# Delta-rule attention, gMLP and rotor mixer on one core: r and u products on four array tiles, a third Gram buffer, masked query parts by DRAM

## The chip, the core and the metric

The kernel runs on one core of a Trainium2 chip. Its engines are TensorE (PE; PEld is its loading of weights), VectorE (DVE), ScalarE (ACT), GpSimd (POOL) and SyncE (SP, which issues the transfers here). The metric is device time of the whole program in microseconds (us), the lower the better; the median of three runs is compared.

## The reference

Three layers follow each other on B=4 sequences of 768 tokens. The first is a delta rule per head (8 heads of 48), which as written goes token by token:

```python
k_n = k / (norm(k) + 1e-06)
for t in range(S):
    y[:, :, t] = q[:, :, t] @ state
    v_old = k_n[:, :, t] @ state
    state += beta * outer(k_n[:, :, t], v[:, :, t] - v_old)
# second: gated MLP; third: token and channel mixing
h = relu(x @ w_in); u, v = split(h); v_n = layernorm(v)
x = (u * (w_spatial @ v_n + b_spatial)) @ w_out
theta = x @ w_theta
y = w_tok_r @ (x * cos(theta)) + w_tok_i @ (x * sin(theta))
u = x + y
out = u + relu(u @ w_ch)
```

## The kernel before

The attention is done in chunks of 64 tokens. A *step* g (0 to 47) is one chunk of one sequence with all 8 heads, four head pairs (`hp`) that lie in partitions 0 to 63 and 64 to 127. Twelve steps make a sequence, eight steps make a *round* r (0 to 5). Per step there are:

- `gram` (L660): the products of the chunk's keys with each other (and, from round 2 on, with its queries) go to PSUM tile `gp`, are multiplied with `gm` (causal mask times beta and norm, made on POOL in `gmask`) on DVE and give `GX` (keys) and `pp` (masked query part). In rounds 0 and 1 the query part is made one step ahead in `jit` (L803), straight into `kq`.
- `norms` (L609), once a round: the norms of the keys, a row of seven small DVE instructions in one task `f2`.
- `invert` (L712), once a round: the 32 unit triangular matrices of the round are inverted together. 30 levels of two DVE instructions (`tmp`, L746; `un`, L758) invert 32x32 blocks after a transpose (L724) and before two (L763, L766); then 32x32 products on PE with PSUM tile `mg` (L784, L790), `MU`=8 matrices at a time, give the blocks below.
- `chain` (L839): PE product r (L858, L859: keys by state `w`), DVE `rt` = r - v (L862), PE product u (L869, L870: inverse by `rt`), two copies to `w`, PE product s (L885, L887: keys by u, summed onto the state), two copies to the next `w`, and PE product y (L897, L898: the output). r, rt, u, s of a step wait for one another, and the next step's r for s.

r and u take 8 matmuls of 64x64 (or 48x64) weights and 48 columns a step. Head 0 of a pair goes to one output half and head 1 to the other, so that two of the four 64x64 tiles of the array are in use. As the operands are fp32, each matmul shows as two records in the trace.

Two buffers `GX` hold the rounds' matrices: round r+2 uses that of round r, so `gram` of step g+16 stands behind `chain` of step g, and `invert` of round r+2 behind the last step of round r.

The big matmuls of the other two layers (`mm_tasks`, L987, recorded at L998) are done for a sequence once its attention is there. A planner (`Plan`) lists all tasks with a priority and assumed durations and writes out every engine's order before the program is built; on the chip each engine runs its list in order and waits on semaphores. It puts big matmuls between the small products of the chain, and where too few are ready it puts in *fillers* (L508): 128x128 transposes whose result is not read, so that TensorE stays busy. They write a corner of PSUM tile `mg`. `park` (L1162) turns the third layer's weights from float64 pairs into fp32 in DRAM, 34 pieces, from step 16 on.

```python
        marks[g] = A(o_pe(480), fu, [rt, G], [pu], pr, crit=True, act=0.312)
```

This line adds the u product as a PE task with an assumed 480 ns.

## Time and profile before

| | |
|---|---|
| median of 3 runs | 806.61 us (800.92 to 808.93) |
| the profiled execution, its own time | 808.53 us |
| its span, first to last instruction | 806.8 us |
| mean granted TensorE clock | 0.972 of 2.4 GHz |
| busy: PE / DVE / ACT / POOL | 749.0 / 583.3 / 399.5 / 148.5 us |
| PE records, DVE instructions | 8947, 1434 |

Busy time is that of the whole span; the kernel has two parts with different limits (steps 0 to 47 of the attention with what fits between, then big matmuls alone), and each has to be read by itself. A busy PE counts the modelled end of each matmul, so neighbouring records overlap; what a group of matmuls takes from PE is read as the distance from its first start to the start of what follows.

### The profile page before, as it was taken

Reading aid. Unit: us, or ns where it says so; the run is one execution under the profiler, and the core shown is the slowest. Engines: PE = TensorE matmul, PEld = TensorE weight load, DVE = VectorE, ACT = ScalarE, POOL = GpSimd, SP = SyncE. Lnnn points to the kernel's source line nnn. Section 1 sums busy time; section 2 is a strip of 40 time slices with the busy share of each in tenths; the row PEclk is TensorE's granted clock in tenths of the full one; section 3 lists DMA queues with packets and bytes.
Section 4 is the critical chain, followed back from the end, with each engine's and each line's share of the span. In section 5 each row is a group of like instructions: output and inputs, shape, how many; then the busy total and the mean of one; then the engine's idle time right before and its main releaser. Section 6 shows DMA issues by size and latency. Waiting matters only on the chain.

```text
span 806.8 us, 21991 instructions
## 1 busy us (share of the span) xinstructions
PE 749.0 (93%) x8947; PEld 684.5 (85%) x8947; DVE 583.3 (72%) x1434; ACT 399.5 (50%) x877; POOL 148.5 (18%) x172
## 2 busy tenths in 40 slices
PE   5486889988998999999899999999999999999998
PEld 4375667867887877888788999999999999999997
DVE  5998998799995699997555544679565575556545
ACT  3836537636555757765777344355333342333321
POOL 2033554243202121211011100012111111111100
PEclk9998989999998999999789999999999999999999
DMA  7615634356387688687764610153010011002001
GB/s 217 221 51 152 195 114 133 106 161 175 113 243 227 200 243 246 188 251 208 210 201 150 216 56 14 67 184 105 22 69 27 27 38 62 24 22 80 1 1 59
DMA packets 84996, 102.42 MB, mean 127 GB/s; under 512 B 8992, under 2 KB 65568, under 8 KB 84896
## 3 DMA queue, kind: packets, MB, share of 16 engines
q1 hardware_dynamic: 84896, 101.03, 41.5%
q8 instruction: 70, 1.15, 0.6%
q14 instruction: 30, 0.25, 0.1%
HBM read 74.38 MB, written 22.41 MB: 120 GB/s over the span
## 4 chain that ended last, share of the span: by engine, by line
PE 69%; DVE 21%; DMA 4%; issue 3%; ACT 3%; SPq 1%; POOLq 0%; DVEq 0%; ACTq 0%
PE m L998 34%; PE y L998 20%; DVE tmp L746 4%; DVE un L758 4%; PE mg L508 3%; PE ru L869 2%; DMA vk<-in_vkn_dram 2%; PE py L897 2%; PE s L885 1%; PE mg L790 1%; PE ru L858 1%; DVE GX L694 1%; DMA k<-in_vkn_dram 1%; PE gp L679 1%; DVE ss L621 1%
## 5 line engine op out<-in xcount | busy, mean ns | idle before, releaser
L998 PE MATMUL m<-w,vh 128*128 128x256 f32 x576 | 111.2, 292 | 2.8 <-issue 1.7
L998 PEld LDWEIGHTS m<-w,vh 128*128 128x128 f32 x576 | 90.3, 193 | 4.4 <-ACT uT L476 1.1
L998 PE MATMUL y<-wr,xTh 128*128 128x384 f32 x432 | 86.2, 337 | 0.0
L998 PE MATMUL m<-w,vl 128*128 128x256 f32 x288 | 82.2, 285 | 1.9 <-DVE vl L930 1.9
L998 PE MATMUL y<-w,xTl 128*128 128x384 f32 x432 | 83.9, 336 | 0.0
L998 PEld LDWEIGHTS y<-wr,xTh 128*128 128x128 f32 x432 | 75.3, 188 | 0.0
L998 PEld LDWEIGHTS y<-w,xTl 128*128 128x128 f32 x432 | 75.1, 188 | 0.0
L758 DVE TENSOR_TENSOR un<-un,tmp 128x30 f32<-128x30 f32 (+21 forms) x209 | 69.1, 342 | 2.0
L746 DVE TENSOR_TENSOR tmp<-un 128x30 f32<-128x30 f32 (+21 forms) x209 | 67.6, 334 | 2.2
L998 PEld LDWEIGHTS m<-w,vl 128*128 128x128 f32 x288 | 55.7, 193 | 3.9 <-DVE vl L930 2.1
L1320 DVE TENSOR_SCALAR bgr<-m 128x384 int32<-128x384 f32 x22 | 12.2, 555 | 56.0 <-PE m L998 56.0
L508 PE MATMUL mg<-ident 128*128 128x128 f32 x274 | 45.3, 310 | 6.0 <-DVE ct L482 2.7
L476 ACT ACTIVATE W<-ru 64x192 f32<-64x192 f32 x84 | 27.3, 325 | 46.0 <-PE ru L870 44.5
L998 PE MATMUL m<-xTh,wih 128*128 128x256 f32 x144 | 47.1, 327 | 0.0
L998 PE MATMUL m<-wo,gh 128*128 128x384 f32 x176 | 44.7, 334 | 0.0
L654 POOL TENSOR_TENSOR gm<-mask,ng 128x256 f32<-128x256 f32 x53 | 36.3, 692 | 37.6 <-DVE pp L709 21.0
L508 PEld LDWEIGHTS mg<-ident 128*128 128x128 f32 x274 | 34.6, 157 | 9.9 <-DVE ct L482 3.3
L998 PE MATMUL m<-xTl,wih 128*128 128x256 f32 x144 | 41.5, 288 | 0.0
L998 PE MATMUL m<-xTh,wil 128*128 128x256 f32 x144 | 41.4, 288 | 0.0
L869 PEld LDWEIGHTS ru<-rt,GX 64*64 64x64 f32 x384 | 27.0, 139 | 15.2 <-DVE rt L862 10.2
L869 PE MATMUL ru<-rt,GX 64*64 64x48 f32 x384 | 32.9, 227 | 7.1 <-DVE rt L862 6.9
L476 ACT ACTIVATE x<-m 128x384 f32<-128x384 f32 x13 | 6.4, 491 | 66.0 <-PE m L998 65.9
(207 smaller groups left out, 2088.3 us busy)
## 6 DMA issues: line engine op xcount, KB each, us to landing
kq<-in_kqT_dram SPq DMA_DIRECT2D x96, 128.0 KB, 3.7
vk<-in_vkn_dram SPq DMA_DIRECT2D x48, 192.0 KB, 3.5
kg<-in_kgT_dram SPq DMA_DIRECT2D x32, 256.0 KB, 3.0
gd<-gt SPq DMA_DIRECT2D x24, 256.0 KB, 3.0
graw<-gd SPq DMA_DIRECT2D x24, 256.0 KB, 2.8
k<-in_vkn_dram SPq DMA_DIRECT2D x24, 192.0 KB, 3.2
xd<-xs SPq DMA_DIRECT2D x48, 96.0 KB, 2.8
xr<-xd SPq DMA_DIRECT2D x24, 192.0 KB, 3.3
```

Source lines behind the costliest of these rows:

```text
L476: nc.scalar.activation(out=out, in_=in_, func=func, **kw)
L508: nc.tensor.transpose(MGt[:, 256:384], ident.t, ident.t)
L621: A(o_dve(192 * KB), lambda e, j=j, k=k: nc.vector.tensor_reduce(out=ss.t[:, j:j + KB], in_=k.t, axis=AX.X, op=ALU.add), [k], [(ss, True)] ...
L654: eng[e].tensor_tensor(out=gm.t, in0=mask.t.unsqueeze(1).to_broadcast([128, HP, CH]), in1=ng_b[r].t[:, j, 1].unsqueeze(2).to_broadcast([12 ...
L679: mm(out=pb()[o:o + 64, hp % 2, hp // 2, :], lhsT=kg.t[i:i + D, 0, hp, :], rhs=kg.t[i:i + D, :, hp, :], start=True, stop=True)
L694: nc.vector.scalar_tensor_tensor(out=GXt[1][:, u0 + hp], in0=GXt[1][:, u0 + hp], scalar=ng_b[1].t[:, j, 1, hp:hp + 1], in1=mask.t, op0=ALU ...
L746: eng[e].tensor_tensor(out=t3, in0=un.t[:, k:k + 1, 0:k].to_broadcast([128, m, k]), in1=un.t[:, t0:32:st, k:k + 1].to_broadcast([128, m, k ...
L758: eng[e].tensor_tensor(out=un.t[:, t0:32:st, 0:k], in0=un.t[:, t0:32:st, 0:k], in1=t3, op=ALU.add)
L869: mm(out=pu.t[64:128, hp, :], lhsT=gx[64:128, u, :], rhs=rt.t[64:128, hp, :], start=True, stop=True)
L897: mm(out=PYt[0:48, hp, q:q + 64], lhsT=w[:, 0, hp, :], rhs=kq.t[:, 1, hp, :], start=True, stop=True)
L998: mm(out=view(), lhsT=a, rhs=c, start=(start and q == 0 and s_ == 0), stop=(stop and q == tot - 1 and s_ == 2))
L1320: P.add(o_dve(DM), lambda e: nc.vector.tensor_scalar(out=ni.t.bitcast(I32), in0=th(), scalar1=1.0 / TWO_PI, scalar2=None, op0=ALU.mult), [ ...
```

## The change

- **r and u on four tiles.** The data layout of heads 0 and 1 of the pairs (`XH`) is swapped against that of 2 and 3, so that one matmul of each of four tiles (straight and crossed) can run side by side; the order is 0, 2, 1, 3, and the two kinds write two PSUM banks (`ru` is now `[128, 2, 512]`). The number of matmuls stays.
- **PSUM.** `mg` is gone; the inversion's products (now `MU`=16 at a time) and the fillers use `gp`.
- **Third Gram buffer** (`NB`=3): `norms`, `gram` and `invert` of round r stand `LG`=5 steps earlier.
- **Masked query parts by DRAM.** `pp` is stored to DRAM at once and loaded from there into `kq` (32 stores more); the ring of `pp` shrinks from 13 to 8. For steps 3 to 15 `jit` writes one 128x256 product to a new tile `jp` and two transfers bring it into `kq`, in place of two 64x256 products straight into `kq`.
- **Round 1 scaled by ACT.** The 32 DVE instructions of 128x64 that scale and mask (L694) become 32 ACT copies with a scale out of PSUM and one DVE mask product of 128x2048.
- **Small DVE rows split.** The seven instructions of `norms` and the six of the layer norm (L1055) become tasks of their own, so that others can stand between. Norms are put into a second place for the swapped heads (`f3`, `f4`).
- `bsp_sb` is loaded in 12 pieces when needed; the second transpose of an inversion is done in place (`un`), behind the first.

```diff
 DYN = ("gp", "gm", "m")
-MU = 8
+XH = (0, 1)
+MU = 16
 WP0 = 0.6
 HVN = 2
 KGN = 2
-PN = 13
+PN = 8
+NB = 3
+JO = 3
+NP1 = -20.25
+LG = 5.0
+LGI = 5
 KQN = 4
 VN = 3
-CTN = 2
+CTN = 1
...
-            nc.tensor.transpose(MGt[:, 256:384], ident.t, ident.t)
+            nc.tensor.transpose(GPt[:, 0:128], ident.t, ident.t)
...
-    bsp_sb = single("pm", "bsp_sb", [128, S])
...
-    GXt = [pools["pa"].tile([128, 32, 64], F32, name=f"GX{i}") for i in range(2)]
-
-    GXc = [[Buf(tile_=GXt[i]) for _ in range(RM)] for i in range(2)]
+    GXt = [pools["pa"].tile([128, 32, 64], F32, name=f"GX{i}") for i in range(NB)]
+
+    GXc = [[Buf(tile_=GXt[i]) for _ in range(RM)] for i in range(NB)]
 
     r_m = ring("ps_m", "m", [128, 512], F32, 2)
-    r_gp = ring("ps_a", "gp", [128, 2, 512], F32, 1)
-    MGt = pools["ps_a"].tile([128, 512], F32, name="mg")
-    r_mg = Fixed(pools, "ps_a", MGt[:, 0:MU * 32].rearrange("p (a b) -> p a b", b=32), "mg")
-    r_ru = ring("ps_a", "ru", [128, HP, D], F32, 1)
+    GPt = pools["ps_a"].tile([128, 1024], F32, name="gp")
+    r_gp = Fixed(pools, "ps_a", GPt, "gp")
+    RUt = pools["ps_a"].tile([128, 2, 512], F32, name="ru")
+    r_ru = Fixed(pools, "ps_a", RUt[:, :, 0:2 * D], "ru")
...
+    r_jp = ring("pa", "jp", [128, HP, CH], F32, 2)
...
+        p0 = (r - 2) * RM + NPR - LG if r > 1 else -20.0 if r == 0 else NP1
...
+        f2 = [lambda e: V.reciprocal(out=n(), in_=sr.t),
+              lambda e: V.tensor_tensor(out=n(), in0=n(), in1=ss.t, op=ALU.mult),
...
+        def f3(e):
+            for p in (0, 64):
+                copy(e, ng.t[p:p + 64, :, 8:10], ng.t[64 - p:128 - p, :, 4:6])
+
+        def f4(e):
+            copy(e, ng.t[:, :, 2:4], sr.t[:, :, 2:4])
+            for p in (0, 64):
+                copy(e, ng.t[p:p + 64, :, 0:2], sr.t[64 - p:128 - p, :, 0:2])
...
+        for f in f2:
+            A(o_dve(32), f, [ss, beta_sb], [ng, sr], p0 + 0.6, crit=r < 2)
+        A([("ACT", 400.0), ("DVE", 250.0)], f3, [ng], [nb], p0 + 0.6, crit=r < 2)
+        ng.readers.extend(nb.writers)
+        A([("ACT", 600.0)], f4, [sr, ng], [nv], p0 + 0.6)
...
+    def slot(hp):
+        return (hp + 2) % HP
...
+            if not fused:
+                for hp in range(HP):
+                    for o in (64, 0):
+                        i = 64 - o
                         kh = kg.t[i:i + D, hp, :]
-                        mm(out=pv()[o:o + 64, hp, :], lhsT=kh, rhs=kh, start=True, stop=True)
+                        ob = 64 - o if hp in XH else o
+                        ib = 64 - ob
+                        kh = kg.t[ib:ib + D, hp, :]
+                        mm(out=pv()[ob:ob + 64, slot(hp), :], lhsT=kh, rhs=kh, start=True, stop=True)
+                return
+            for hp in (2, 3):
+                for o in (64, 0):
+                    i = 64 - o if hp == 2 else o
+                    c0 = 384 + 128 * (hp - 2)
+                    mm(out=GPt[o:o + 64, c0:c0 + 2 * CH], lhsT=kg.t[i:i + D, 0, hp, :], rhs=kg.t[i:i + D, :, hp, :], start=True, stop=True)
+            for hp in XH:
+                for w, c0 in ((0, 640 + 128 * hp), (1, 192 + 128 * hp)):
+                    for i in (0, 64):
+                        o = i if w == 0 else 64 - i
+                        mm(out=GPt[o:o + 64, c0:c0 + CH], lhsT=kg.t[i:i + D, 0, hp, :], rhs=kg.t[i:i + D, w, hp, :], start=True, stop=True)
...
-            A([("ACT", d_actp(256))], lambda e: act(GXt[1][:, u0:u0 + HP, :], pv(), ACTF.Copy), [ps], [GXc[1][j]], pr, port=False)
-
             def fs4(e):
-                for hp in range(HP):
-                    nc.vector.scalar_tensor_tensor(out=GXt[1][:, u0 + hp], in0=GXt[1][:, u0 + hp], scalar=ng_b[1].t[:, j, 1, hp:hp + 1],
-                                                   in1=mask.t, op0=ALU.mult, op1=ALU.mult)
-
-            A([("DVE", 4 * d_dve(64))], fs4, [ng_b[1], mask], [GXc[1][j]], G1P)
+                for q in range(HP):
+                    act(GXt[1][:, u0 + q], pv()[:, q], ACTF.Copy, scale=ng_b[1].t[:, j, 6 + q:7 + q])
+
+            A([("ACT", 4 * 170.0)], fs4, [ps, ng_b[1], nb_b[1]], [GXc[1][j]], pr, port=False)
+            ng_b[1].readers.append(P.tasks[-1])
+            if j == RM - 1:
+                A([("DVE", d_dve(2048))], lambda e: nc.vector.tensor_tensor(
+                    out=GXt[1], in0=GXt[1], in1=mask.t.unsqueeze(1).to_broadcast([128, 32, CH]), op=ALU.mult),
+                  [mask], GXc[1], G1P, after=inv0)
...
+            pd = pp_b[g] = Buf(tile_=pools["dram"].tile([128, HP, CH], F32, name=f"pp{g}"))
+            A(dma(131072), lambda e: nc.sync.dma_start(out=pd.t, in_=pp.t), [pp], [pd], pr + PMP, extra=2000.0)
...
+        xt = Buf()
+        A([("DVE", 1900.0)], lambda e: nc.vector.transpose(out=un.t.rearrange("p u s -> p s u"),
+                                                           in_=un.t.rearrange("p t s -> p s t")),
+          ub, [xt, un], pr + 0.1, crit=cr, port=False)
...
+            kq, ps = kq_b[g], r_m.new()
...
+            if g >= JO:
+                pp = r_jp.new()
+                A(o_dve(256), lambda e: nc.vector.tensor_tensor(out=pp.t, in0=gpv(ps), in1=gm.t[:, 0:HP], op=ALU.mult),
+                  [ps, gm], [pp], pr, port=False, after=inv0)
+                for p0, i in ((64, 1), (0, 2)):
+                    A(dma(65536), lambda e, p0=p0, i=i: nc.sync.dma_start(out=kq.t[p0:p0 + 64, i], in_=pp.t[p0:p0 + 64]),
+                      [pp], [(kq, True)], pr, extra=LOADLAT)
...
-                for hp in range(HP):
-                    mm(out=ps.t[64:128, hp, :], lhsT=kq.t[0:48, 0, hp, :], rhs=w[0:48, 0, hp, :], start=True, stop=True)
-                    mm(out=ps.t[0:64, hp, :], lhsT=kq.t[64:112, 0, hp, :], rhs=w[64:112, 1, hp, :], start=True, stop=True)
-
-            kq.readers.append(A(o_pe(490), fr, [kk_b[g]] + ws, [ps], pr, crit=True, act=0.235))
-            A(o_dve(192), lambda e: nc.vector.tensor_tensor(out=rt.t, in0=ps.t, in1=v.t[:, 0], op=ALU.subtract),
+                for hp in (0, 2, 1, 3):
+                    h, q = divmod(hp, 2)
+                    for a in (0, 1):
+                        o = 64 * a if hp in XH else 64 - 64 * a
+                        mm(out=ps.t[o:o + 64, h, q * D:(q + 1) * D], lhsT=kq.t[64 * a:64 * a + D, 0, hp, :], rhs=w[64 * a:64 * a + D, a, hp, :],
+                           start=True, stop=True)
+
+            kq.readers.append(A(o_pe(270), fr, [kk_b[g]] + ws, [ps], pr, crit=True, act=0.47))
...
-                mm(out=pu.t[64:128, hp, :], lhsT=gx[64:128, u, :], rhs=rt.t[64:128, hp, :], start=True, stop=True)
-                mm(out=pu.t[0:64, hp, :], lhsT=gx[0:64, u, :], rhs=rt.t[0:64, hp, :], start=True, stop=True)
-
-        marks[g] = A(o_pe(480), fu, [rt, G], [pu], pr, crit=True, act=0.312)
-        A(o_cpp(192), lambda e: copy(e, w[64:128, 0], pu.t[64:128]), [pu], [wu[0]], pr, crit=True, port=False, part=64)
-        A(o_cpp(192), lambda e: copy(e, w[0:64, 1], pu.t[0:64]), [pu], [wu[1]], pr, crit=True, port=False)
+            for hp in (0, 2, 1, 3):
+                h, q = divmod(hp, 2)
+                for a in (0, 1):
+                    o = 64 - 64 * a
+                    i = 64 - o if hp in XH else o
+                    mm(out=pu.t[o:o + 64, h, q * D:(q + 1) * D], lhsT=gx[i:i + 64, j * HP + slot(hp), :], rhs=rt.t[i:i + 64, hp, :],
+                       start=True, stop=True)
+
+        marks[g] = A(o_pe(260), fu, [rt, G], [pu], pr, crit=True, act=0.62)
...
+        if fp == 0:
+            bs_b[b, h3] = r_bs.new()
+            load(bs_b[b, h3], lambda t=bs_b[b, h3]: t.t, b_sp[:, t0:t1], 131072, pr)
...
+    ahead = {}
+    for r in range(2, NR):
+        for j in range(RM):
+            ahead.setdefault(max(0, (r - 2) * RM + j - LGI), []).append((r, j))
...
+        for r2, j2 in ahead.get(g, ()):
+            p2 = (r2 - 2) * RM + j2 - LG
+            if j2 == 0:
+                norms(r2)
+            gram(r2 * RM + j2, p2 + GPR)
+            if j2 == RM - 1:
+                invert(r2, p2 + IPR)
```

The planner then writes another order. In the order written for the change, big matmuls that took 127.7 us before (at the spacings of rows 4) stand ahead of the last y product as 96.2 us; there are 352 fillers and one more transpose where there were 274; 21 of the 34 pieces of `park` stand ahead of the last `rt` on DVE where all 34 did. 37 rows of fillers wait on a semaphore (23 on DVE) where 16 did.

DVE where the inversion of round 2 ends and that of round 3 begins. Before (`GX_111` and `GX_112` are the two Gram buffers; `nb`, `td` are the layer norm's small steps):

```order
L758 TENSOR_TENSOR un<-un,tmp 128x30
L1056 RECIPROCAL nb<-sd 128x2
L1057 TENSOR_TENSOR td<-td,nb 128x2
L1058 TENSOR_TENSOR td<-td,sd 128x2
L1059 TENSOR_SCALAR td<-td 128x2
L1060 RECIPROCAL td<-td 128x2
L1061 TENSOR_TENSOR nb<-mv,td 128x2
L763 STREAM_TRANSPOSE xt_3309<-un 128x32x32
L766 STREAM_TRANSPOSE GX_111<-un 128x32x32
L930 TENSOR_TENSOR vl<-hv,vh 128x512
L724 STREAM_TRANSPOSE un<-GX_112 128x1024
```

and in the change (three buffers, `GX_110` to `GX_112`; the step's `rt` is step 16's):

```order
L791 TENSOR_TENSOR un<-un,tmp 128x30
L795 STREAM_TRANSPOSE GX_112<-un 128x32x32
L736 TENSOR_TENSOR GX_111<-gp,gm 128x256
L800 STREAM_TRANSPOSE un<-un 128x32x32
L740 TENSOR_TENSOR pp<-gp,gm 128x256
L910 TENSOR_TENSOR rt<-ru,vk 128x192
L875 TENSOR_TENSOR vk<-vk,ng 128x384
L1097 TENSOR_SCALAR mv<-sm 128x1
L981 TENSOR_TENSOR xTl<-xr,xTh 128x3x128
L1105 TENSOR_SCALAR td<-mv 128x2
```

The row of small steps stands behind the inversion, and a Gram of a later round stands between its two transposes.

PE between the u and the s product of step 24, with what waits. Before (`gp<-kg` is a Gram, `m<-xTh,wih` and the like are big matmuls, `s<-W` is s):

```order
L679 MATMUL gp<-kg 64x128 [waits DMAHW5_49]
L679 MATMUL gp<-kg 64x128 x7
L998 MATMUL m<-xTh,wih_141 128x256
L998 MATMUL m<-xTl,wih_141 128x256
L998 MATMUL m<-xTh,wil_144 128x256
L998 MATMUL m<-xTh,wih_139 128x256
L998 MATMUL m<-xTl,wih_139 128x256
L998 MATMUL m<-xTh,wil_142 128x256
L998 MATMUL m<-xTh,wih_140 128x256
L998 MATMUL m<-xTl,wih_140 128x256
L998 MATMUL m<-xTh,wil_143 128x256
L885 MATMUL s<-W_109,vk 48x48 [waits DVE_49]
```

and in the change, from the u product (`ru<-rt,GX`) on; L514 are fillers, L824 is an inversion's product:

```order
L920 MATMUL ru<-rt,GX_110 64x48 [waits Pool_49] x2
L920 MATMUL ru<-rt,GX_110 64x48 x6
L514 MATMUL gp<-ident 128x128 [waits Activation_49]
L514 MATMUL gp<-ident 128x128 x7
L824 MATMUL gp<-GX_110,ct 32x32 x32
L514 MATMUL gp<-ident 128x128
L936 MATMUL s<-W_108,vk 48x48 [waits Activation_49]
L938 MATMUL s<-W_108,vk 48x48 [waits Activation_49]
```

Nine big matmuls stood in the gap; in the change fillers and an inversion's product stand there.

PE between r and u of step 25 in the change (`ru<-W` is r):

```order
L906 MATMUL ru<-W_109,kq 64x48 [waits DMAHW4_49,DVE_49]
L906 MATMUL ru<-W_109,kq 64x48 [waits DMAHW5_49,Activation_49]
L906 MATMUL ru<-W_109,kq 64x48 x6
L514 MATMUL gp<-ident 128x128 [waits DVE_49]
L514 MATMUL gp<-ident 128x128 x6
L920 MATMUL ru<-rt,GX_110 64x48 [waits DVE_49]
```

The first filler now waits for DVE, since the PSUM tile that it writes is the Gram's and DVE reads it.

## Rows read from the trace of the kernel before

**Rows 1.** The page, part 1: busy us (share of the span) and instructions.
```profile
PE 749.0 (93%) x8947; PEld 684.5 (85%) x8947; DVE 583.3 (72%) x1434; ACT 399.5 (50%) x877; POOL 148.5 (18%) x172
```
**Rows 2.** Windows: length, busy us (instructions) of five engines, clock, DMA share, GB/s.
```profile
0.00:210.10 210.10, 165.97 (x2857) 139.84 (x2857) 184.95 (x542) 112.18 (x269) 72.51 (x94) 0.95 0.50 146
210.10:277.20 67.10, 63.12 (x1216) 53.99 (x1215) 49.60 (x129) 41.45 (x89) 10.65 (x15) 0.95 0.72 218
277.20:337.80 60.60, 57.70 (x1004) 48.39 (x1002) 57.77 (x155) 41.95 (x88) 14.50 (x17) 1.00 0.75 222
337.80:393.00 55.20, 52.02 (x933) 44.65 (x925) 47.02 (x124) 34.62 (x75) 7.28 (x8) 0.99 0.82 238
393.00:440.80 47.80, 47.80 (x672) 39.58 (x672) 23.07 (x63) 34.09 (x79) 5.84 (x4) 0.84 0.61 182
440.80:806.80 366.00, 362.42 (x2283) 358.10 (x2282) 220.85 (x425) 135.15 (x279) 37.71 (x35) 1.00 0.18 60
```
**Rows 3.** Timeline of PE: first record of u in steps 16, 24, 32, 40, 46, 47.
```profile
210.10 0.25 PE L869 MATMUL ru<-rt,GX 64*64 64x48 f32 x1
...
277.17 0.25 PE L869 MATMUL ru<-rt,GX 64*64 64x48 f32 x1
...
337.84 0.25 PE L869 MATMUL ru<-rt,GX 64*64 64x48 f32 x1
...
392.95 0.34 PE L869 MATMUL ru<-rt,GX 64*64 64x48 f32 x1
...
435.45 0.25 PE L869 MATMUL ru<-rt,GX 64*64 64x48 f32 x1
...
440.80 0.25 PE L869 MATMUL ru<-rt,GX 64*64 64x48 f32 x1
```
**Rows 4.** Timeline of PE: big matmuls, a u product, a Gram, an inversion product.
```profile
292.33 0.28 PE L998 MATMUL m<-xTl,wih 128*128 128x256 f32 x1
292.44 0.28 PE L998 MATMUL m<-xTh,wil 128*128 128x256 f32 x1
...
302.70 0.40 PE L998 MATMUL m<-wih,xTl 128*128 128x512 f32 x1
302.93 0.39 PE L998 MATMUL m<-wih,xTh 128*128 128x512 f32 x1
...
297.96 0.25 PE L869 MATMUL ru<-rt,GX 64*64 64x48 f32 x1
...
298.35 0.22 PE L869 MATMUL ru<-rt,GX 64*64 64x48 f32 x1
298.41 0.22 PE L869 MATMUL ru<-rt,GX 64*64 64x48 f32 x1
...
298.56 0.39 PE L998 MATMUL m<-xTh,wih 128*128 128x256 f32 x1
...
299.46 0.67 PE L679 MATMUL gp<-kg 48*64 48x128 f32 x16
...
143.66 0.69 PE L790 MATMUL mg<-GX,ct 32*32 32x32 f32 x32
```
**Rows 5.** Groups by line, DVE: busy us, mean ns of one, idle before.
```profile
L758 DVE TENSOR_TENSOR un<-un,tmp 128x30 f32<-128x30 f32 (+21 forms) x209 | 69.1, 342 | 2.0
L816 DVE TENSOR_TENSOR kq<-gp,gm 64x256 f32<-64x256 f32 x32 | 13.4, 419 | 2.2 <-PE gp L812 1.6
L694 DVE SCALAR_TENSOR_TENSOR GX<-GX,ng,mask 128x64 f32<-128x64 f32 x32 | 8.7, 347 | 0.0
```
**Rows 6.** The chain that ended last, in order of time: start, us, what.
```profile
199.45 1.82 DVE GX L766
...
381.12 7.56 DMA vk<-in_vkn_dram
...
443.68 58.57 PE m L998 x438
502.25 3.13 PE y L998 x18
```
**Rows 7.** Waits of PE: who for whom, us in total, times, longest.
```profile
PE mg L508 <- DVE ct L482: 2.7, 2, 1.8
PE mg L508 <- ACT GX L476: 2.6, 3, 0.9
...
PE mg L508 <- ACT ct L476: 0.5, 2, 0.3
```
**Rows 8.** DMA issues: count, KB each, median us from issue to landing.
```profile
kq<-pp SPq DMA_DIRECT2D x64, 64.0 KB, 3.3
```

More of the change, by code (lines that the diff above doesn't have):

```diff
@@ new lines, in f3 @@
+        def f3(e):
[5 more added lines that the diff above has]
+                copy(e, ng.t[p:p + 64, :, 0:2], sr.t[64 - p:128 - p, :, 0:2])
+        nb = nb_b[r] = Buf(tile_=ng)
+        nv = nv_b[r] = Buf(tile_=ng)
+        A([("DVE", 90.0)], f1, [ss], [ss], p0 + 0.6, crit=r < 2, after=gate)
+        A([("ACT", 120.0)], lambda e: act(sr.t, ss.t, ACTF.Sqrt), [ss], [sr], p0 + 0.6, crit=r < 2)
@@ L806, in jit @@
         if r < FUSE:
-            kq, ps = kq_b[g], r_gp.new()
+            kq, ps = kq_b[g], r_m.new()
             def f(e):
@@ L972, in load_w1 @@
                           l, lambda l=l, c=c: l.t[:, c:c + 256], pr)
-        load(bsp_sb, lambda: bsp_sb.t, b_sp, 393216, 4)
         for i in range(NT):
```

188 lines of the change are left out of this document (88 added, 100 removed).

## The prediction

> **What bounds the kernel now.** I read the page's busy shares first: PE 93%, DVE 72% [rows 1]. They say that PE is the limit, but they mix two parts. The windows cut at the u products of steps 16, 24, 32, 40 and 47 [rows 2, 3] part them. From 440.8 us, the u of step 47, to the end at 806.8 PE is busy for 362.42 of 366.00 us, and the chain of waits runs through big matmuls alone [rows 6]: that part is PE-bound and costs what is left of the big work. Before it DVE is the fuller engine: 184.95 of 210.10 us up to step 16, 57.77 of 60.60 between steps 24 and 32, 47.02 of 55.20 between 32 and 40. PE looks as full there, but a big share of its busy time is the modelled ends of short matmuls and fillers. Only in steps 40 to 47 is DVE half idle (23.07 of 47.80) while PE is full, at a mean clock of 0.84 of 2.4 GHz. So the end is the time of step 47 plus the big work that is left then. Both move in this change, in opposite directions.
>
> **Big work pushed behind the attention.** By the order, big matmuls worth 127.7 us stood ahead of the last y product and 96.2 us do now, at starts 0.11 to 0.12 us apart for 256 columns, 0.23 for 512 [rows 4] and 3.13/18 = 0.174 for 384 [rows 6]. The last part so grows by 31.5 us; its big work of 351.5 us took 366.0, transposes and switches included, so I take 32. The change gains only if step 47 comes more than 32 us earlier.
>
> **r and u on four tiles.** Of a u product, the first record starts at 297.96, the last at 298.41 and the next work at 298.56 [rows 4]: 0.60 us, of which 0.46 are 8 pairs of records, 0.06 apart, two tiles side by side. Four tiles make 4 groups of four. The Gram of round 2 and later already uses four tiles and two PSUM banks: 16 records of 128 columns end after 0.67 us, one lasting 0.27, so that 16 starts take about 0.40 [rows 4] although each moves 128 columns and not 48. And 32 records of an inversion end after 0.69 us [rows 4], which is 0.015 a start once the 0.2 of a last record is off. Sixteen starts so cost 0.23 to 0.25; the saving is 0.21 us a product, 0.42 a step. 92 products are 19 us of PE, but only where PE is waited for. Bounds: nothing, and 0.23.
>
> The Trainium skill speaks against this in "TensorE: Matmul & The Clock Gate" (section "Wait — 56ns, not 53.3ns?"): start-to-start never drops below about 25 ns however small N is. By it 16 starts would keep 0.40 of the 0.46 us, and the 92 products would give back 5.5 us, an estimate by that page. The trace disagrees: the 32 records above start 0.015 us apart.
>
> **DVE load.** I multiplied each DVE instruction of both orders by the mean time of its kind. This load counts overlaps twice, so I use its ratio to the busy time of the same window. Up to the last `rt` it falls from 413 to 370 us. About 16 of the 43 us are work that vanishes: the 32 scalings of 8.7 us [rows 5] become one product of 2048 columns, which no row shows: by the 342 ns of a mean `un` step [rows 5] as a bound below and eight times a 256-column product of 0.42 as one above it is 0.3 to 3.4 us, and I take 2.3, near the upper since the columns count; the 32 `kq` products of 13.4 us [rows 5] become 19 of the same length, 8 us; copies that go to ACT give 5. The rest, some 27 us, is second-layer and `park` work pushed behind step 47, where DVE is busy for 220.85 of 366.00 us [rows 2] and takes it unseen. If that cover were gone, it would cost up to 27 us.
>
> **The stages.** (a) To step 16. The third inversion ends on DVE at 199.45 + 1.82 = 201.3 [rows 6], and u of step 16 follows at 210.10, after copies and PE products. The load ahead of that end is 199.7 before and 190.8 now; times 184.95/199.7 that is -8 us. The half-inversions of 16 matrices make each link behind it longer, but halve their number; I leave it at nothing, bounds -1 and +3. (b) Steps 16 to 24, 67.1 us. The fourth inversion stood in one piece behind the third and loads DVE with 47.9 us up to the `rt` of step 20, now 39.1: -8. Steps 20 to 24 are PE-bound; four steps by 0.42 give -2. (c) Steps 24 to 32, 60.7 us: load 65.7 to 46.3, times 57.77/65.7 = -17. That leaves 43.6 us for 8 steps, 5.4 each, as step 47 follows step 46 by 5.35 [rows 3], so it is not below what the chain has shown. (d) Steps 32 to 40, 55.1 us: load 56.2 to 50.0, times 47.02/56.2 = -5. A load of `vk` of 7.56 us is on the chain here [rows 6], with DMA engines 82% busy [rows 2]. Thirteen of 34 `park` pieces (384 KB in, 192 KB out each) leave this part, some 7 MB, and the stores of `pp`, the `jp` copies and the `bs` pieces add 7 MB, mostly earlier: I take -3 for the stall. (e) Steps 40 to 47: 7 by 0.42 = -3. Sum: -8 -10 -17 -8 -3 = -46, so u of step 47 falls at 394.8 us.
>
> **Costed at nothing.** The ACT scaling adds 32 small copies, at most 0.35 us each, less 8 that go, about 8 us before step 1; ACT is half idle [rows 1], and the first inversion on DVE covers it. Masks of 384 columns on POOL: by 1.5 times, about 12 us more on an engine 18% busy [rows 1]. `pp` to DRAM: stored 13 or more steps before use; a landing takes 3.3 us [rows 8] against 5 us a step. `jp` for steps 3 to 15: y now waits for a transfer with the next r behind it on PE; in DVE's order `jp` stands ahead of its step's `rt` in each case, which covers most of 3.3 us. Uncovered, 13 of these cost 43 us. Small DVE rows cost the same singly; a row of six blocked DVE for about 1.2 us and no longer does. `bs` pieces: 12 loads of 128 KB in a part with DMA 18% busy.
>
> **Sum.** 394.8 + 366.0 + 32 = 792.8 us of span. The profiled execution took 808.53 us for a span of 806.8, 1.7 around it, and lies 1.9 above the median 806.61. So the median of the change should be 792.8 + 1.7 - 1.9 = 792.6, say 793 us, 1.7% less.
>
> **The rivals.**
> *No use for the freed time* (chance 0.20). Steps may be held by latencies and by the in-order PE list, not by DVE's load; stage (c) then gives 4 us and not 17, the stall of (d) stays: step 47 at 411, 809 us. For it: DVE is idle for 17.5 us in steps 16 to 24 [rows 2] and the chain still takes its time. Against: the fullest stages lose most load.
> *Fillers that wait* (slower, 0.17). Fillers now share the Gram's PSUM tile; 37 of them wait and 23 of those for DVE, with r, u or s queued behind on PE. Before, those on `mg` idled PE for 2.7 + 2.6 + 0.5 us in 7 waits, the longest 1.8 [rows 7]. At 1.0 each 37 cost 37 us, 31 of them new: 793 + 31 = 824. From 0.75 us each on, 28 in all and 22 of them new, the change is slower by over 1%. For it: DVE is the full engine. Against: most such gaps end in an r or u that waits for DVE anyway.
> *The stalls go too* (0.16). With a round's inversion 5 steps earlier the idle of stage (b) may vanish: 17.5 us of DVE idle, of which I counted 2. Then about 776 us.
> *A start floor* (0.03). If records cannot start closer than the 0.03 us of today's u product, four tiles give nothing: the 2 us of (b) and the 3 of (e) go, 798 us. For it only that no 48-column product on four tiles is in the trace; against it the Gram and the inversion [rows 4]. The Trainium skill's 25 ns, cited above, comes near this case.
> My forecast, 784 to 801 us, has 0.44.
>
> **Chances.** About 1% is what a measurement of this kernel tells from no change: faster is below 798.5 us, slower above 814.7. Faster: most of 0.44, the 0.16 and half of 0.03, 0.58. Same: the remainder of the forecast and most of the no-use case, 0.24. Slower: 0.18. The range that leaves 2 in 10 out is 773 to 815 us; the likeliest case's own is 784 to 801.
>
> **What would show it.** Right: a u product taking about 0.37 us to the next start; u of step 16 near 202 and of step 47 near 395 us; solid big matmuls for about 398 us after it; DVE still above 85% busy to step 36. Wrong: waits of fillers for DVE or ACT above 20 us in sum; y waiting for `kq` from `jp` for microseconds; a clock below 0.8 over long stretches where fillers replaced big matmuls; or step 47 later than 409 us.

## The result, and the profile after

The change is slower: 811.15 us median (804.95 to 817.34, 20 executions) against 804.34 (795.66 to 813.02) for the kernel before on the same chip, ratio 1.0101, 95% interval 1.0066 to 1.0136. The forecast was 793.0, faster by 1.7%. The profiled execution spans 811.0 us (before 806.8). Every ratio below is to runs of the kernel before on the same chip as that experiment; its median there lies between 800.5 and 804.3. A ratio leaves out executions in the chip's slower state and is not the quotient of the medians beside it.

The starts of the u products, from the timelines of PE, show by stage where forecast and trace part. Two more columns are experiments that follow below; every column but the forecast is one execution.

| us | before | forecast | after | after, no fillers | before, no fillers |
|---|---|---|---|---|---|
| u of step 16 | 210.1 | 202.1 | 196.1 | 188.6 | 213.9 |
| 16 to 24 | 67.1 | 57.1 | 66.5 | 57.3 | 62.5 |
| 24 to 32 | 60.7 | 43.6 | 58.2 | 53.8 | 61.2 |
| 32 to 40 | 55.1 | 47.1 | 45.9 | 51.6 | 52.3 |
| 40 to 47 | 47.8 | 44.8 | 44.0 | 41.1 | 43.0 |
| u of step 47 | 440.8 | 394.8 | 410.7 | 392.5 | 432.9 |
| from there to the end | 366.0 | 398.0 | 400.3 | 401.3 | 366.1 |

Windows of after, cut at these products (length, busy us of PE, PEld, DVE, ACT and POOL with instructions, granted clock, DMA share, GB/s); they answer to [rows 2]:

```profile
0.00:196.09 196.09, 150.88 (x3087) 128.30 (x3087) 166.02 (x501) 114.66 (x288) 70.20 (x89) 0.94 0.64 181
196.09:262.63 66.54, 55.62 (x1145) 48.84 (x1140) 46.82 (x122) 28.31 (x60) 16.66 (x18) 0.87 0.70 202
262.63:320.79 58.16, 51.31 (x992) 42.38 (x992) 43.97 (x106) 30.18 (x57) 11.93 (x11) 0.85 0.57 167
320.79:366.71 45.92, 45.76 (x881) 37.00 (x880) 41.27 (x126) 36.67 (x85) 11.73 (x12) 1.00 0.79 221
366.71:410.73 44.02, 41.76 (x693) 36.91 (x687) 21.29 (x45) 26.20 (x52) 2.10 (x2) 0.92 0.72 219
410.73:811.00 400.27, 395.08 (x2499) 387.59 (x2498) 250.20 (x503) 164.21 (x336) 41.75 (x37) 1.00 0.24 78
```

DVE has lost load (43.97 us busy between steps 24 and 32, 57.77 before), but from 16 to 32 the time has hardly moved (124.7 us, 127.7 before). Neither engine is full there any more, and the clock, 0.95 and 1.00 in [rows 2], is 0.87 and 0.85. The groups of the page name what grew, the fillers (out<-in, count | busy, mean ns | idle before and what ended it), first of before, then of after:

```profile
L508 PE MATMUL mg<-ident 128*128 128x128 f32 x274 | 45.3, 310 | 6.0 <-DVE ct L482 2.7 <-ACT GX L476 2.6 <-ACT ct L476 0.5
```
```profile
L514 PE MATMUL gp<-ident 128*128 128x128 f32 x352 | 63.3, 327 | 24.3 <-DVE pp L740 8.1 <-DVE GX L736 6.8 <-ACT ct L482 5.6
```

PE stood idle 24.3 us in front of fillers, 6.0 before. The waits of PE in after that make up nearly all of it, 23 of them, where [rows 7] had 7 (total, times, longest):

```profile
PE gp L514 <- DVE pp L740: 8.1, 7, 2.1
...
PE gp L514 <- DVE GX L736: 6.8, 6, 2.2
...
PE gp L514 <- ACT ct L482: 5.6, 6, 1.3
...
PE gp L514 <- ACT GX L482: 3.3, 4, 1.3
```

Of the 24.3 us, 15.2 lie ahead of the u of step 16, which came early, and 9.1 behind it (the same group up to 196.09 us, and from there on):

```profile
L514 PE MATMUL gp<-ident 128*128 128x128 f32 x217 | 37.3, 320 | 15.2 <-DVE pp L740 8.1 <-DVE GX L736 3.3 <-ACT ct L482 2.6
L514 PE MATMUL gp<-ident 128*128 128x128 f32 x135 | 25.9, 339 | 9.1 <-DVE GX L736 3.5 <-ACT ct L482 2.9 <-ACT GX L482 2.5
```

The worst place lies between the u products of steps 23 (242.06 us) and 25 (274.32), where before took 9.4 us (and after without fillers, E2 below, 19.4). The chain of after there, in order of time (start, us, what):

```profile
244.68 2.64 PE gp L514 x15
...
249.37 1.16 PE gp L818 x64
...
250.55 0.59 ACT ct L482
...
251.15 0.60 ACT ct L482
...
251.79 2.48 PE gp L514 x13
254.28 1.87 PE gp L824 x64
...
256.17 0.59 ACT GX L482
...
256.77 0.60 ACT GX L482
...
257.41 3.04 PE gp L514 x13
260.45 1.85 PE gp L818 x64
```

This is the tail of the fourth inversion. L818 is the product of a piece of 16 matrices; ACT copies it to `ct` by 251.75, and L824 could start then. In PE's order 13 fillers stand between. They were meant to run during the copies, but write the tile that the copies read, so they start when the copies end and then hold PE for 2.48 us. The same happens after GX. The u of step 24 (262.63) stands behind the L818 of the second piece.

### The profile page after: what moved, and what is told of

It is laid out like the page before. It is cut to its first block, busy times and chain, and to the rows that moved or that the text cites. A ratio compares the mean times of both kernels' runs of the same rounds, so it can differ in the third digit from the quotient of the medians.

```text
span 811.0 us, 22761 instructions
## 1 busy us (share of the span) xinstructions
PE 740.4 (91%) x9281; PEld 681.0 (84%) x9281; DVE 569.6 (70%) x1398; ACT 400.2 (49%) x878; POOL 154.4 (19%) x169
## 4 chain that ended last, share of the span: by engine, by line
PE 64%; DVE 17%; DMA 6%; ACT 5%; issue 5%; SPq 2%; POOL 1%; POOLq 0%; DVEq 0%; ACTq 0%
PE m L1050 30%; PE y L1050 19%; PE gp L514 6%; DVE un L791 4%; DVE tmp L779 4%; DMA k<-in_vkn_dram 2%; DMA xr<-xd 2%; PE gp L824 1%; PE py L948 1%; DVE GX L736 1%; PE gp L818 1%; ACT ct L482 1%; PE s L936 1%; PE ru L920 1%; PE m L1357 1%
## 5 line engine op out<-in xcount | busy, mean ns | idle before, releaser
L514 PE MATMUL gp<-ident 128*128 128x128 f32 x352 | 63.3, 327 | 24.3 <-DVE pp L740 8.1
L514 PEld LDWEIGHTS gp<-ident 128*128 128x128 f32 x352 | 47.9, 166 | 30.5 <-DVE pp L740 10.0
L791 DVE TENSOR_TENSOR un<-un,tmp 128x30 f32<-128x30 f32 (+21 forms) x209 | 71.0, 350 | 1.5
L671 POOL TENSOR_TENSOR gm<-mask,ng 128x384 f32<-128x384 f32 (+1 forms) x52 | 43.2, 836 | 56.3 <-DVE pp L740 26.3
L482 ACT ACTIVATE W<-ru 64x192 f32<-64x192 f32 x87 | 28.4, 326 | 45.9 <-PE ru L920 43.4
L1050 PE MATMUL m<-xTh,wih 128*128 128x256 f32 x144 | 43.6, 303 | 0.9 <-ACT hv L482 0.9
L482 ACT ACTIVATE W<-s 48x192 f32<-48x192 f32 x78 | 25.6, 328 | 26.2 <-PE s L938 25.0
L1050 PE MATMUL m<-uh,wc 128*128 128x384 f32 x144 | 38.5, 337 | 0.0
```

Source lines behind the costliest of these rows:

```text
L482: nc.scalar.activation(out=out, in_=in_, func=func, **kw)
L514: nc.tensor.transpose(GPt[:, 0:128], ident.t, ident.t)
L671: eng[e].tensor_tensor(out=gm.t[:, lo:hi], in0=mask.t.unsqueeze(1).to_broadcast([128, hi - lo, CH]), in1=ng_b[r].t[:, j, 4 + lo:4 + hi].un ...
L791: eng[e].tensor_tensor(out=un.t[:, t0:32:st, 0:k], in0=un.t[:, t0:32:st, 0:k], in1=t3, op=ALU.add)
L1050: mm(out=view(), lhsT=a, rhs=c, start=(start and q == 0 and s_ == 0), stop=(stop and q == tot - 1 and s_ == 2))
```

## Experiments

**Fillers: moved, left out, and left out of the kernel before.** My theory A was that fillers wait for readers of the Gram tile and then hold PE in front of the chain. Theory B was that the third buffer's order makes the stalls and fillers only fill them. Theory C was that the clock decides.

E1 moves them, and moves the inversion's products to columns 512 to 1023 (the second edit is not shown here):

```
-            nc.tensor.transpose(GPt[:, 0:128], ident.t, ident.t)
+            nc.tensor.transpose(GPt[:, 0:128] if fl[0] else RUt[:, 0, 256:384], ident.t, ident.t)
```
(`fl[0]` is set by r and u, and cleared by the s or y of the same step.) E2 and E3 leave them out, of after and of before:
```
-        for _ in range(n):
+        for _ in range(n if n == BURST0 else 0):
```

> The changed kernel in the same order, but the fillers write where fewer readers are pending: into unused columns of the r/u tile whenever the last r or u product has been read, else into the first bank of the Gram tile; the products of the inversion write the second bank of that tile. In the order 19 fillers wait for another engine instead of 37. Theory A (fillers wait for readers of the Gram tile and then hold PE in front of the chain): the idle before fillers falls from 24 us to below 10, the two runs of 13 fillers between the half-inversions of round 4 start at the end of the product before them, u of step 25 comes at 262 to 268 instead of 274.3, and the kernel takes 790 to 800 us. Theory B (the stalls come from where the third Gram buffer's order has put the inversion, and fillers only fill time in which the chain waits for something else): 808 to 813 us. Theory C (clock): the granted clock between steps 24 and 25 stays at 0.6 and with it the time, 808 to 813 us.

> The changed kernel in the same order without its fillers (transposes whose result nobody reads; the first burst of 60 stays). Theory A: 24 us of waits and what the fillers hold PE for are gone, against a colder clock in some steps: 785 to 805 us. Theory B: the chain does not get faster, 808 to 815 us. Theory C (the clock is what decides, and fillers carry it): step 47 comes later than 420 us, 820 us or more.

> Control: the kernel before in its own order without its fillers (results that nobody reads; the burst of 60 stays). Theory A: only 6 us of waits stood before its fillers, so that little is won and some clock is lost, 800 to 815 us, and the kernel without fillers of the change comes out ahead of this one by 10 us or more. Theory B: leaving out fillers changes before and after alike, and after stays behind. Theory C: 820 us or more here too.

Measured: E1 800.0 us, ratio 0.9999 (0.9961 to 1.0038); E2 793.05, 0.9867 (0.9795 to 0.9939); E3 797.86, 0.994 (0.9895 to 0.9984). Moving fillers takes 1.0% off, leaving them out 2.3%; in the kernel before that is worth only 0.6%. In E1's profile 188 records, the burst among them, now write `ru` and wait for nobody:

```profile
L516 PE MATMUL ru<-ident 128*128 128x128 f32 x188 | 29.8, 305 | 0.0
L516 PE MATMUL gp<-ident 128*128 128x128 f32 x164 | 28.9, 315 | 14.9 <-DVE GX L738 5.5 <-DVE pp L742 5.0 <-ACT ct L482 3.8
```

Idle before fillers fell to 14.9 us and not below 10 as A had it, but u of step 25 came at 261.6 us, earlier than A asked. E3 misses A too: it came out 2 us below the range, and the change without fillers is ahead of it by 5 us and not 10. B fell with E2, whose 793 us lie 15 below its range. For theory C, the windows of that stretch, u of step 23 to u of step 25, in after, in E14 (below; its fillers wait as in after), E1 and E2:

```profile
242.10:274.30 32.20, 26.46 (x441) 22.57 (x441) 9.62 (x24) 10.29 (x18) 4.76 (x5) 0.61 0.53 154
```
```profile
241.70:266.54 24.84, 18.39 (x441) 15.77 (x442) 9.92 (x24) 10.36 (x18) 4.66 (x5) 0.93 0.63 183
```
```profile
240.11:261.56 21.45, 18.07 (x442) 15.44 (x442) 9.81 (x24) 10.35 (x18) 3.98 (x4) 0.92 0.72 217
```
```profile
234.01:253.37 19.36, 13.41 (x377) 12.08 (x377) 9.69 (x24) 9.36 (x17) 3.71 (x4) 0.50 0.79 230
```

Without fillers the granted clock is 0.50, its 1.2 GHz level throughout, and the stretch is the shortest; moved fillers hold it at 0.92 and gain nothing over that. So a cold clock alone does not make the stall, but it has a share in its length: E14 has the order and the waits of after there, and at 0.93 takes 24.8 us where after at 0.61 takes 32.2. Thirteen fillers behind the same wait, in after and in E14:

```profile
251.79 2.48 PE L514 MATMUL gp<-ident 128*128 128x128 f32 x13 [1.29 <-ACT ct L482]
```
```profile
251.43 1.64 PE L514 MATMUL gp<-ident 128*128 128x128 f32 x13 [1.29 <-ACT ct L482]
```

Of the 10.8 us by which E1 is shorter there than after, 7.4 thus go with the clock and 3.4 with the tile that the fillers write, in these single executions. In the whole time the tile counts at a like clock too: at a mean clock of 0.97 or more, after took 806.0 to 811.4 us (six executions), E14 805.5 to 807.0 (three) and E1 798.7 to 800.2 (six), on chips where before had medians of 804.3, 801.7 and 802.1.

The Trainium skill, in "TensorE: Matmul & The Clock Gate", section "Part 4: PE-mode transpose", says that the fast clock does not engage for transposes in PE's transpose mode. This trace does not agree, if the fillers run in that mode, which it does not show (they appear as plain MATMUL): the same order shows 0.92 with them in E1 and 0.50 without in E2.

**Which of them, and which sharing.** E5 leaves fillers out between the u of step 23 and that of step 25 alone. E9 keeps only those that E1 writes to `ru`. E14 keeps all and puts only the inversion's products into the other bank. E16 puts the fillers of the kernel *before* on free columns of its Gram tile (declared once, for that).

```
E5   for _ in range(0 if fl[0] in (23, 24) else n):      # fl[0]: step of the last u
E9   for _ in range(n if n == BURST0 or fl[0] is None else 0):
E14  -pv = GPt[:, 256:256 + MU * 32]...    +pv = GPt[:, 1024 - MU * 32:1024]...
E16  -transpose(MGt[:, 256:384], ...)   +transpose(GPt[:, 0, 256:384], ...)
```

> The changed kernel in the same order, without the fillers that are issued between the u products of steps 23 and 25 (65 records, 14.8 us of PE there; nobody reads their results), all other fillers kept. Theory A (fillers in the tail of round 4's inversion wait for the copies of the products and then hold PE before the next product): the stretch between these two products falls from 32.2 to about 20 us, as in the two runs without or with moved fillers (19.4 and 21.5), and most of the 12 us reaches the end: 798 to 803 us. Theory B (the stretch is set by the inversion's own links): it stays above 28 us, 807 to 812.

> The changed kernel in the same order with only those fillers that in the moved version write the r/u tile, none of which waits for another engine; the others (results that nobody reads) are left out, the burst of 60 stays. If waiting is what fillers cost: the idle before them is zero and the time that of no fillers at all or better through the clock, 786 to 795 us. If holding PE costs as much: between moved fillers and none, 796 to 801 us, with the chain still passing through fillers.

> The changed kernel with all its fillers in the same order; only the products of the inversion write the second bank of the Gram tile (columns 512 to 1023) and not columns 256 to 767, so that fillers, in the first bank, no longer share one with them. If it is this bank that makes fillers wait for the copies ct and GX (5.6 and 3.3 us of 24 us idle in the profile) and then hold PE before the next piece: the stretch from step 23's u to step 25's falls from 32.2 to 22 to 26 us and the time to 800 to 806 us. If waits for the Gram's readers on DVE decide: 807 to 812 us.

> One part alone: the kernel before in its own order, with its fillers on unused columns of the Gram tile's first bank instead of the inversion's tile. 18 of them wait for another engine in the order, against 16. If sharing a bank with the Gram is what made the fillers of the change costly: the idle before fillers rises from 6 to 15 us or more, 808 to 816 us. If it is sharing with the larger inversion pieces, and more fillers: 800 to 806 us.

E5: 804.05 us, 1.0011 (0.9967 to 1.0055). 65 records in one stretch cost 0.9%, some 7 us, and the stretch took 19.3 us, as theory A had it; the time is 1 us above that theory's range. E9: 798.95, 0.9976 (0.9939 to 1.0014): as E1, so the 164 records that E1 has beyond it, with all of the 14.9 us that PE is idle before them, cost nothing clear of noise. E9's interval touches E2's, lies above that of E10 and overlaps that of E18 (all three without fillers), so what fillers that wait for nobody cost by holding PE is not settled. E14: 810.02, 1.0103 (1.0055 to 1.0152), no change in time. The stretch from step 23's u to step 25's did fall to 24.8 us, which I had expected if it was the bank, but its waits are those of after:

```profile
PE gp L514 <- DVE pp L740: 8.1, 8, 2.2
...
PE gp L514 <- DVE GX L736: 7.5, 6, 2.3
PE gp L514 <- ACT ct L482: 6.0, 6, 1.3
...
PE gp L514 <- ACT GX L482: 3.5, 5, 1.3
```

The fillers (columns 0 to 127) wait for copies that read columns 512 to 1023 of the same tile, in another bank, as long as ever. The wait belongs to the tile as the program tracks it, so my expectation was on a false footing, and moving fillers helped only where it was to another tile, as in E1. The shorter stretch goes with the clock of 0.93: E4 below, with its products where after has them, took 25.1 us there at 0.93 as well. E16: 813.2, 1.0125 (1.0085 to 1.0165). One tile name changed in the old kernel costs as much as the whole change. Its waits, of a profiled execution at the long end (824.09 us):

```profile
PE gp L508 <- DVE kq L817: 16.8, 7, 5.6
...
PE gp L508 <- DVE pp L710: 2.9, 4, 1.4
```

There it is the `kq` products on DVE, which the change takes off that tile, that they wait for most, and nearly all of that execution's loss lies ahead of step 16 (its u at 224.8 us, 210.1 before). So E16 shows what a tile with other readers can cost, but not at the place where the change loses.

**Two array tiles.** E4 undoes the order of the heads with fillers, E10 without.

```
-for hp in (0, 2, 1, 3):
+for hp in (0, 1, 2, 3):
```

> The changed kernel with the heads of r and u in the order 0, 1, 2, 3 instead of 0, 2, 1, 3: two array tiles at a time as before, all else in the same order. The u product should go from 0.45 back to about 0.66 us. If r and u are on the path that sets the end only where PE is waited for (my forecast), 92 products cost about 5 us: 815 to 818. If every one is on the path, 19 us: 828 to 832. If the chain waits elsewhere throughout, 810 to 813.

> The changed kernel without fillers (results that nobody reads), in the same order, with r and u on two array tiles at a time (heads 0, 1, 2, 3). To compare with the run without fillers (793.05 us). With fillers the two tiles cost nothing measurable (ratio 1.0095 against 1.0101). If fillers hid it: my forecast's 5 us, 796 to 801. If the chain does wait for more than these 0.2 us at every product: the same as without, 789 to 797. If all 92 products are on the path: 810.

E4: 811.9, 1.0095 (1.0051 to 1.0139); E10: 793.67, 0.9888 (0.9849 to 0.9927). Both equal their counterparts, after and E2. But the u product did not go back to 0.66 us. In after, then E10 (timeline: start, duration):

```profile
400.18 0.45 PE L920 MATMUL ru<-rt,GX 64*64 64x48 f32 x16
400.56 0.51 PE L1050 MATMUL m<-w,vh 128*128 128x256 f32 x2
```
```profile
384.64 0.46 PE L920 MATMUL ru<-rt,GX 64*64 64x48 f32 x16
385.04 0.50 PE L1050 MATMUL m<-w,vh 128*128 128x256 f32 x2
```

The next work follows after 0.38 us in one and 0.40 in the other, where [rows 4] had 0.60. So the 0.22 us are there, but the head order is not what gives them, and these runs do not show what the saving is worth. Which of the rest of the edit gives it (two PSUM banks, heads 0 and 1 on the other pair of tiles) was not tried.

**The other parts, without fillers.** E7, E8, E11, E12 and E13 leave fillers out as E2 and E3 do. Each of the seven changes the planned order too.

```
E6   FILL_END = 470000.0 -> 0.0 (the planner, too, knows of no fillers)
E7   NB = 3 -> 2, LG = 5.0 -> 0.0, LGI = 5 -> 0
E8   MU = 16 -> 8, CTN = 1 -> 2
E11  JO = 3 -> 48
E12  MU = 16 -> 32, PN = 8 -> 6, pieces at columns 0 to 1023
E13  kernel before: MU = 8 -> 16, CTN = 2 -> 1
E15  pieces as E12, FILL_END as E6
```

> The changed kernel with the planner told to use no fillers, so that they are neither issued nor counted in its model; the order of all engines changes. If the order was good and fillers alone were the fault: as without them in the old order, 788 to 797 us. If the planner, seeing a colder clock, pulls big matmuls into the attention: step 47 later than 400 us but less left behind it, 785 to 800 us. If it loses the clock: above 805.

> The changed kernel without fillers (results that nobody reads) and with two Gram buffers instead of three and Gram and inversion of a round at their old due times; the order is planned anew. To compare with the run without fillers (793.05 us). If the third buffer gave the shorter stage between steps 16 and 24 (57.3 us there against 62.5 in the kernel before without fillers): 62 us or more again, and 797 to 805 us. If it only moved the wait from one round's start to another: 789 to 797 us. If it costs: below 789.

> The changed kernel without fillers (results that nobody reads) and with the inversion's products in four pieces of 8 matrices and two copies buffers again instead of two of 16; planned anew. To compare with the run without fillers (793.05 us). If the long pieces make each round's start wait (step 24's u 12.0 us after step 23's, step 32's 10.4 after step 31's): these gaps fall by 2 to 4 us each, 786 to 791 us. If the number of links decides: 793 to 800 us. My forecast put this edit at nothing, -1 to +3 us per inversion.

> The changed kernel without fillers (results that nobody reads) and without the jp copies: steps 3 to 15 multiply into kq on DVE directly, two products each, as the kernel before does in steps 0 to 15; planned anew. To compare with the run without fillers (793.05 us). My forecast took 5 us of DVE in steps 1 to 16 off and the wait of y for the copy as hidden: step 16 later by 3 to 6 us, 795 to 799. If the copies' wait costs: 786 to 792. If DVE was not the limit there: 790 to 796.

> The changed kernel without fillers (results that nobody reads) and with the inversion's products in one piece of 32 matrices instead of two of 16 (and 6 pp buffers instead of 8, for the room); planned anew. Pieces of 8 cost 12 us against pieces of 16. If the number of links between PE and ACT at each inversion's end decides: step 16 and the rounds' starts earlier again, 783 to 790 us. If a round's first step now waits for a whole piece that it does not need: its start later by 3 to 5 us each, 795 to 808 us.

> One part alone: the kernel before without fillers (results that nobody reads) and with the inversion's products in two pieces of 16 matrices and one copy buffer; planned anew. To compare with the kernel before without fillers (797.86 us, ratio 0.994). If the number of links between PE and ACT at the end of each inversion is what the pieces of 16 save, as the change with pieces of 8 suggested (12 us): 785 to 791 us. If that difference came from the new order of the big matmuls: 794 to 802 us.

> Towards a better kernel: pieces of 32 matrices, and a planner told to use no fillers (6 pp buffers instead of 8). Pieces of 32 in an order planned with fillers gave 782.33 us without them. If the gain is that of fewer links: 776 to 788 us, with step 47 earlier than 419. If it came from that one order, in which more big matmuls stand inside the attention: 788 to 797 us.

Each new plan put another number of big matmuls ahead of step 47, so that step's time says little by itself. The counts are those of the windows of the big products' line alone (x after the busy time), here before and E12:

```profile
0.00:440.80 440.80, 168.69 (x918) 129.34 (x918) 0.95 0.62 183
440.80:806.80 366.00, 359.39 (x2179) 348.92 (x2178) 1.00 0.18 60
```
```profile
0.00:418.98 418.98, 173.99 (x990) 137.67 (x990) 0.85 0.67 197
418.98:777.70 358.72, 351.27 (x2107) 340.15 (x2106) 1.00 0.23 75
```

At the end a record costs 366.00/2179 = 0.168 us. The last column, an estimate, takes that times the count off step 47's time: what the attention costs beside the big work done in it.

| | us | ratio (95%) | u of step 47 | big ahead | rest |
|---|---|---|---|---|---|
| before | 804.34 | 1 | 440.8 | 918 | 287 |
| after | 811.15 | 1.0101 (1.0066 to 1.0136) | 410.7 | 702 | 293 |
| E3 before, no fillers | 797.86 | 0.994 (0.9895 to 0.9984) | 432.9 | 918 | 279 |
| E2 after, no fillers | 793.05 | 0.9867 (0.9795 to 0.9939) | 392.5 | 702 | 275 |
| E6 planned without | 792.57 | 0.9913 (0.9876 to 0.9949) | 400.4 | 780 | 269 |
| E7 two Gram buffers | 804.3 | 1.0045 (1.0009 to 1.0081) | 395.8 | 690 | 280 |
| E8 pieces of 8 | 805.05 | 1.0077 (1.0039 to 1.0115) | 430.2 | 879 | 283 |
| E11 no jp | 803.74 | 1.0041 (1.0007 to 1.0076) | 396.8 | 714 | 277 |
| E12 pieces of 32 | 782.33 | 0.9753 (0.9667 to 0.9838) | 419.0 | 990 | 253 |
| E13 before, pieces of 16 | 810.03 | 1.0093 (1.0059 to 1.0128) | 423.9 | 834 | 284 |
| E15 pieces of 32, planned | 787.39 | 0.9824 (0.976 to 0.9889) | 419.3 | 924 | 264 |

Undoing the third buffer, the pieces of 16 or `jp` each loses 1.8 to 2.1% against E2 (ratio by ratio, each with its new plan), so that none of these parts shows as the fault. The mechanisms that I had expected mostly missed. E8, E11 and E13 took longer than every case that I gave. E7's time is that of "the third buffer gave the shorter stage", but its steps 16 to 24 took 55.6 us and not 62 or more; it lost between 32 and 40, 59.5 us for E2's 51.6. E12 beats both kernels, the one before by 2.5%, with step 16 at 218.3 us, 30 later than in E2 and not earlier. E15's time fits fewer links, its step 47, no earlier than E12's, does not. Whether the pieces do it by fewer links between PE and ACT is open. On the kernel before (E13) pieces of 16 brought step 47 forward by 9.0 us against E3, as that idea wants, but 84 fewer big matmuls stood ahead of it, 14 us, and the kernel lost 1.5%. The size of a piece cannot be told from the order that the planner makes with it.

**The transpose in place.** In after, DVE's first step of the fifth inversion waits for the fourth's last product, which reads `un`, a wait that my sum did not hold; in before the product read a tile of its own.

```profile
DVE un L757 <- PE gp L818: 14.1, 1, 14.1
```

E17 gives the transposed matrices a tile of their own from the fourth inversion on, in the same order; E18 does so without fillers.

```
+xv = (lambda: XTt.rearrange("p (u s) -> p u s", s=32) if r > 2 else un.t)
...
-out=un.t.rearrange("p u s -> p s u")    +out=xv().rearrange("p u s -> p s u")
...
-rhs=un.t[q:q + 32, u0 + u, :]           +rhs=xv()[q:q + 32, u0 + u, :]
```

> The changed kernel with fillers, in the same order on every engine; only the second transpose of an inversion from round 4 on (counting from 1) writes a tile of its own and not un in place (it shares the room of the two jp buffers, used up by then; 6 pp buffers instead of 8 in fact). In the changed kernel DVE's first step of the next inversion waits 14.1 us, at 248 to 262, for PE's last product of the inversion before, which reads un. If that wait delays the chain: the third windows' start, u of step 32, comes 6 to 12 us earlier than 320.8, and the time is 799 to 806 us. If DVE has room to catch up before step 32: nothing, 808 to 813 us.

> The same tile, without fillers (results that nobody reads). To compare with the run without fillers (793.05 us), where the same wait was 8.0 us. If the wait delays the chain: 785 to 789 us, u of step 32 at 292 to 296 instead of 299.8. If not: 790 to 796 us.

E17: 816.2 us, 1.0174 (1.0095 to 1.0253), E18: 796.5, 0.9932 (0.9889 to 0.9974): no gain in either. The u of step 32 came at 324.9 us (320.8 in after) and 298.0 (299.8 in E2). The wait is gone and DVE idles at the next row of its order, here in E18 between steps 24 and 32:

```profile
DVE W L488 <- PE s L943: 11.6, 2, 8.9
```

The copy of `s` waits for the product behind the inversion's tail on PE. That the tail sets this stretch and DVE's wait only shows it fits these rows, but was not tested by itself. The theory that the wait costs time fell.

## Why the prediction was wrong

**The step that failed** is the price of the fillers. The sum has no term for them, and "Fillers that wait" stood in the prediction with its 37 waits and a chance of 0.17, set aside because "most such gaps end in an r or u that waits for DVE anyway". E2 shows what they cost: 19 us in the change (1.0101 against 0.9867) and 5 in the kernel before (0.6%); E4 against E10 and E17 against E18 differ by 2.1 and 2.4% again. These 14 us turn a kernel 0.7% faster than its counterpart without fillers into one 1.0% slower. The rival counted waits alone, 31 us, of which 24.3 - 6.0 = 18 came. That 793 + 18 makes 811, the time measured, is luck: waits are not the price by themselves. The 14.9 us of them left in E1 cost nothing clear of noise (E9). At the tail of one inversion, with 5.7 us of waits, 65 fillers cost some 7 us (E5): a filler that is late there also holds PE in front of the next product, and longer at the clock that after had there (2.48 us for 13, 1.64 in E14). I gave the holding no term. How the 19 us divide among waiting, holding and clock stays open.

**The sum without that rival** was close in its total. It gave step 47 at 394.8 us, 398 behind it and 793; E2 shows 392.5, 401.3 and 793.05. Luck has a part in this: against before E2 is faster by 1.3% (0.6 to 2.1), where 1.7 was forecast, and the stages agree less well than their sum. In E2 step 16 came 13.5 us earlier than forecast, and 24 to 32 took 10.2 longer.

(a) To step 16: 8 us less forecast, 14 measured (196.1 for 210.1). Kernels with one order up to there reached it between 191.0 (E5) and 199.9 us (E17), and E4, which differs in the order of heads alone, at 203.9, so the 6 us are not far out of the spread. But the working was low: DVE was busy for 184.95 us up to there in [rows 2] and is for 166.02 now, 18.9 less and not 8. (b) 16 to 24: 57.1 forecast, 66.5 measured, 57.3 without fillers. From step 16 to 23 after and E2 are alike (46.0 and 45.4 us); the stretch behind made the difference. My working had it half wrong all the same. It took 8 us from DVE's load in the stage, but DVE was busy for 49.60 us there in [rows 2] and is for 46.82 now. (c) 24 to 32: 43.6 forecast, 58.2 measured, 53.8 without fillers. Here a term was mis-sized apart from fillers: 17 us forecast, 7 came without them. Scaling 60.6 by DVE's load assumed that DVE sets the stage, but [rows 2] had PE busy for 57.70 of 60.60 us, as full as DVE, and I had put that down to modelled ends and fillers. No filler lay in that window of before (PE and PEld, L508 alone):

```profile
277.20:337.80 60.60, 0.00 (x0) 0.00 (x0) 1.00 0.75 222
```

The same stage in E2, in E1, and E1's fillers in it:

```profile
245.98:299.77 53.79, 46.42 (x922) 40.20 (x918) 45.13 (x102) 30.16 (x57) 11.92 (x11) 0.66 0.67 202
```
```profile
254.13:306.46 52.33, 46.01 (x993) 38.49 (x992) 43.34 (x102) 29.76 (x57) 11.16 (x11) 0.97 0.70 208
```
```profile
254.13:306.46 52.33, 11.78 (x74) 7.87 (x73) 0.97 0.70 208
```

E2's PE is busy for 46.42 us at a clock of 0.66; at 0.97 E1's is for 46.01, of which 11.78 are fillers. DVE is busy for 45.13 and 43.34. Neither is full any more, and the stage still takes 52 to 54 us, so the load of DVE does not set it alone. What does is not shown. (d), (e): 47.1 and 44.8 forecast, 45.9 and 44.0 measured: right in size (51.6 and 41.1 in E2).

**Big work behind step 47**: 32 us more forecast, 34.3 measured: right. **r and u on four tiles**: 0.21 us forecast and 0.22 measured a product. The Trainium skill's rule in "TensorE: Matmul & The Clock Gate", section "Wait — 56ns, not 53.3ns?", that starts keep about 25 ns apart, left 0.06 us of saving. By this case's traces it doesn't hold across tiles: 64 records of L818 take 1.16 us above, 0.018 each. **Costed at nothing**: that y waits for `jp` costs nothing to be seen; the waits of after for it are 0.2 us in all, and leaving it out was no faster (E11).

```profile
PEld py L948 <- DMA kq<-jp: 0.2, 1, 0.2
```

Missed was the transpose in place, which costs nothing either (E17, E18).

**"No use for the freed time"** named step 47 at 411 and 809 us, and the trace shows 410.7 and a span of 811.0. The numbers agree, the mechanism only in part: without fillers step 47 comes at 392.5 us, so that freed time is used, but stage (c) gave 7 of its 17 us, and there this rival was partly right. Of the signs of being wrong three came: the waits of fillers, the clock (0.61 in the stall) and step 47.

## What to carry to other kernels

A filler is work with a place and a tile: when its output tile changes, list who reads that tile, since each reader can make the filler late, and a late filler holds the in-order engine in front of what it was to bridge. Time the kernel without its fillers before arguing about anything else. Where two engines are full in a stage, a saving on one need not shorten it by as much: in (c) DVE's busy time fell by 12.6 us in E2 and the stage by 7. Where a planner makes the order, count the work done ahead of a landmark as well as its time: E12 reaches step 47 26.5 us later than E2 and ends 16 us earlier in the profiled executions (11 by the medians).
